# Landmarks of q and k from summed tokens: VectorE and GpSimd ahead of 16 small products, and a new order table

## The chip, the cores and the metric

The kernel runs on one core of one Trainium2 chip. The metric is the device time of one execution in microseconds, as the median of several runs. The core's engines are TensorE (PE; its weight loads are PEld), VectorE (DVE), ScalarE (ACT), GpSimd (POOL) and SyncE (SP), which work side by side, each through its own queue in order; 16 DMA engines move data.

## The reference

Eight batches of eight heads go through a Nystrom attention, and its output, 4608 rows of 512, through an MLP with squared relu. S is 576, D is 64, and m, the number of landmarks, is 32: each landmark is the mean over 18 neighbouring tokens.

```
q_lm = q.reshape(B, H, m, S // m, D).mean(axis=3)
k_lm = k.reshape(B, H, m, S // m, D).mean(axis=3)
A = sm(q, k_lm); Bm = sm(q_lm, k_lm); C = sm(q_lm, k)      # softmax of scaled scores
Z = Bm.T / (norm1(Bm) * norminf(Bm) + 1e-06)
for _ in range(6):
    Z = 2 * Z - Z @ Bm @ Z
x = (A @ Z @ C @ v)            # then heads side by side: rows of 512
out = square(maximum(x @ w_in, 0)) @ w_out                  # w_in 512x2048, w_out 2048x512
```

## The kernel before

**Layout.** A batch's q and k are loaded as bfloat16 into one buffer `kqraw`, with 96 partitions and six neighbouring tokens of each head on each partition (`c` in `[96, 2, 8, 6, 64]`); the next batch's load needs that buffer free. v has two buffers. From batch 2 on (`late`) a DMA transposition issued by SP (L420) makes `kqT` from the whole of `kqraw`; batches 0 and 1 transpose on TensorE. After the transposition a copy of one element (`seen`, L330) on GpSimd waits for it, and GpSimd then issues the load of v. All loads of q, k, v and the weights are issued by GpSimd (L331, L339, L347); stores and transpositions by SP.

**Landmarks.** Batch 0 makes them with `means` (L437) and `fold_mm`. Every later batch uses `means2` (L475): 48 products per batch with the band matrix `seg` as the weights, in groups of 32 columns; an eviction with a scale into `lmk`; `fold2_mm` (L492), four products with `ident` that bring them to the head dimension; and evictions into `kbd` (twice) and `dups["q"]`. `b_mm` (L544) makes the landmark scores in eight products that each use a quarter of the array's columns, and a softmax and six iterations follow: in each, GpSimd masks (`mask`, L579), TensorE multiplies (`step`, L640) and VectorE updates (`upd`, L651). `c_mm` (L680) and `a_mm` (L782) make the other scores. `cv_mm` (L731) takes v, `wt_mm` joins, and `g_mm` (L853) multiplies with w_in to G; with A (normalised in `a_mul`, L817, on GpSimd or VectorE), G gives the MLP's hidden layer directly.

**MLP.** `mlp_in` has 16 blocks per batch: four products (L873), a `relu` out of PSUM on ScalarE (L889) or VectorE (L891), and a `square` on ScalarE (L898) or VectorE (L900). `mlp_out` has 592 output products in all (L931), 16 to an accumulation, each then copied and stored.

**Order.** Nothing runs in the order in which it is written. `add` only records an operation with its possible engines, a cost in nanoseconds, what it reads and writes. The table `ORDER`, made ahead by a planner from these costs, is then walked by `emit`: an entry holds the operation's number (entry // 40), the engine (entry // 8 % 5: PE, ACT, DVE, POOL, SP) and the PSUM bank (entry % 8). A negative entry is a fill: products of zeros (L394), in units of 64 columns. So the costs given to `add`, the `dma=` figures among them, change nothing on the chip by themselves; what runs on which engine and in which order is in the table alone. An engine that waits for a semaphore holds up all that its queue has behind.

```
code, bank = divmod(code, 8)
idx, e = divmod(code, 5)
op, e = self.ops[idx], self.ENGINES[e]
```

Of the kernel before, what the change touches and what calls it, by code (L numbers as in the profile page):

```python
# [8 lines left out]
P = 128  # L9
# [8 lines left out]
H = 8  # L18
S = 576
# [213 lines left out]
def kernel(  # L233
# [165 lines left out]
    def constants3(e):  # L399
        nc.vector.memzero(kbd[:])  # L400
        nc.vector.memzero(cvd[:])
        for i in range(2):
            nc.vector.memzero(ECs[i][:, :, :, :, TP:P])
            nc.vector.memzero(kqTs[i][:, 2 * HT:2 * HT + M])

    add({"DVE": (1000.0,)}, constants3, writes=["kbd0", "kbd1", "cvd"])
    add({"DVE": (900.0,)}, constants2, reads=["ident", "onesf"], writes=["fold", "ones"])

    load("v", 0)

# [589 lines left out]
```

## Time and profile before

| | |
|---|---|
| time, median of 3 runs | 260.7 us (259.63 to 267.23) |
| profiled execution, its own time | 261.31 us |
| its span, first to last instruction | 259.6 us |
| granted TensorE clock | 0.999 |
| busy PE / DVE / ACT / POOL | 248.1 / 184.1 / 178.4 / 84.3 us |
| HBM read, written | 36.70 MB, 9.44 MB |

Busy time of TensorE comes from modelled ends of products that overlap, so its pace is better read from the distance between starts of products in a run. The chain of waits follows the last instruction back to what released it. A group's row gives the sum and the mean of its instructions, then the idle time of their engine just ahead of them and what ended it.

### The profile page before, as it was taken

What the parts mean: (1) busy time and instruction counts of PE and PEld (TensorE: products, weight loads), DVE (VectorE), ACT (ScalarE), POOL (GpSimd) and SP (SyncE); (2) the same over time, 40 slices, a digit from 0 to 9 for tenths busy, and PEclk for the clock granted to TensorE, in tenths of its full rate; (3) what the DMA queues carried; (4) which work ended last, traced back from release to release, by engine and by line L of the source; (5) the groups of instructions that cost most, each with busy time, mean ns of one, the idle gap of its engine ahead of it and who ended that gap; (6) DMA issues with size and microseconds to landing.
All of it is one profiled execution on the core that took longest, in us unless ns stands there. A gap on an engine that the chain in (4) does not pass through costs nothing.

```text
span 259.6 us, 7149 instructions
## 1 busy us (share of the span) xinstructions
PE 248.1 (96%) x2910; PEld 144.2 (56%) x2910; DVE 184.1 (71%) x428; ACT 178.4 (69%) x352; POOL 84.3 (32%) x127
## 2 busy tenths in 40 slices
PE   8999999999999999996999799999999999999994
PEld 2755756655555656453564376556655555645543
DVE  2289879589866997788678688887777776684300
ACT  1398988788944996786895588899857375436402
POOL 6154752604333423521474227113523530000000
PEclk9999999999999999999999999999999999999999
DMA  6999999798997999999899998989661633100405
GB/s 80 203 199 207 196 200 204 115 210 129 206 226 138 147 178 216 229 156 191 159 183 193 214 182 143 206 137 197 173 110 13 121 81 130 40 3 0 163 8 197
DMA packets 72753, 39.46 MB, mean 152 GB/s; under 512 B 45456, under 2 KB 68240, under 8 KB 72720
## 3 DMA queue, kind: packets, MB, share of 16 engines
q0 software_dynamic: 23040, 18.35, 48.0%
q1 hardware_dynamic: 49536, 20.58, 36.6%
q8 instruction: 23, 0.38, 0.6%
q14 instruction: 10, 0.08, 0.1%
q10 hardware_dynamic: 144, 0.07, 0.1%
HBM read 36.70 MB, written 9.44 MB: 178 GB/s over the span
## 4 chain that ended last, share of the span: by engine, by line
PE 66%; DMA 23%; POOL 3%; DVE 2%; issue 2%; ACT 2%; DVEq 0%; POOLq 0%; ACTq 0%
PE ps L931 37%; PE ps L873 18%; DMA kqraw<-in_q_dram 9%; DMA kqraw<-in_k_dram 7%; DMA kqT<-kqraw 4%; DMA w_out_bf<-in_moe_w_out_dram 3%; PE ps L394 3%; PE ps L853 3%; PE ps L475 1%; POOL EA L817 1%; PE ps L782 1%; PE ps L521 1%; PE ps L640 1%; POOL Pd L579 1%; PE ps L731 1%
## 5 line engine op out<-in xcount | busy, mean ns | idle before, releaser
L931 PE MATMUL ps<-w_out_bf,gs 128*128 128x512 bf16 (+2 forms) x592 | 146.8, 374 | 0.6 <-DMA w_out_bf<-in_moe_w_out_dram 0.6
L931 PEld LDWEIGHTS <-gs 128*128 128x128 bf16 x592 | 53.5, 98 | 45.2 <-issue 4.3
L873 PE MATMUL ps<-AT,G 128*128 128x288 bf16 x512 | 78.3, 286 | 0.0
L889 ACT ACTIVATE r<-ps 128x576 bf16<-128x576 f32 x88 | 54.9, 652 | 28.9 <-PE ps L873 24.5
L873 PEld LDWEIGHTS <-G 128*128 128x128 bf16 x512 | 48.3, 98 | 23.4 <-issue 0.4
L579 POOL TENSOR_TENSOR Pd<-st,ones_d 128x256 bf16<-128x256 bf16 x42 | 30.4, 725 | 70.0 <-DVE st L651 53.3
L898 ACT ACTIVATE gs<-r 128x576 bf16<-128x576 bf16 x65 | 43.9, 684 | 3.3 <-DVE r L891 2.8
L891 DVE TENSOR_SCALAR r<-ps 128x576 bf16<-128x576 f32 x40 | 30.0, 752 | 15.8 <-PE ps L873 14.2
L900 DVE TENSOR_TENSOR gs<-r 128x576 bf16<-128x576 bf16 x63 | 30.4, 494 | 4.3 <-ACT r L889 3.6
L265 ACT COPY o<-ps 128x512 f32<-128x512 f32 (+2 forms) x29 | 16.2, 571 | 14.0 <-PE ps L931 13.9
L265 ACT CAST G<-ps 128x512 bf16<-128x512 f32 x39 | 21.2, 589 | 6.2 <-PE ps L853 6.0
L817 POOL TENSOR_TENSOR EA<-EA,rA 96x384 bf16<-96x384 bf16 x20 | 16.7, 848 | 17.1 <-DVE rA L810 12.8
L651 DVE SCALAR_TENSOR_TENSOR st<-st,ps 128x128 bf16<-128x128 bf16 x40 | 11.3, 281 | 15.3 <-PE ps L640 13.7
L267 DVE CAST G<-ps 128x512 bf16<-128x512 f32 x25 | 16.8, 684 | 3.2 <-PE ps L853 3.1
L791 DVE TENSOR_REDUCE mxA<-ps 96x16 f32<-96x512 f32 x24 | 16.3, 680 | 0.9 <-PE ps L782 0.7
L800 ACT ACTIVATE EA<-SA 96x512 bf16<-96x512 f32 x24 | 14.7, 627 | 2.6 <-issue 2.1
L794 DVE TENSOR_TENSOR SA<-ps,mxA 96x512 f32<-96x512 f32 x24 | 16.1, 676 | 0.3
L394 PE MATMUL ps<-zero 128*128 128x512 bf16 (+5 forms) x48 | 14.6, 431 | 1.3 <-DVE zero L389 1.3
L806 DVE TENSOR_REDUCE sA<-EA 96x24 f32<-96x768 bf16 x16 | 14.8, 932 | 0.0
L691 ACT ACTIVATE EC<-ps,nmc 128x576 bf16<-128x576 f32 x16 | 11.8, 743 | 1.1 <-DVE nmc L686 1.0
L686 DVE TENSOR_REDUCE nmc<-ps 128x1 f32<-128x576 f32 x16 | 11.7, 748 | 1.0 <-PE ps L680 0.8
L579 POOL TENSOR_TENSOR BTd<-BTc,ones_d 128x256 bf16<-128x256 bf16 x7 | 4.7, 669 | 21.7 <-DVE BTc L267 15.7
(110 smaller groups left out, 240.6 us busy)
## 6 DMA issues: line engine op xcount, KB each, us to landing
out_dram<-o SPq DMA_DIRECT2D x35, 256.0 KB, 3.0
kqraw<-in_k_dram POOLq DMA_DIRECT2D x8, 576.0 KB, 7.2
kqraw<-in_q_dram POOLq DMA_DIRECT2D x8, 576.0 KB, 11.4
vraw<-in_v_dram POOLq DMA_DIRECT2D x8, 576.0 KB, 8.5
w_in_bf<-in_moe_w_in_dram POOLq DMA_DIRECT2D x4, 512.0 KB, 9.9
w_out_bf<-in_moe_w_out_dram POOLq DMA_DIRECT2D x4, 512.0 KB, 10.1
out_dram<-o SPq DMA_DIRECT2D x1, 192.0 KB, 2.3
kqT<-kqraw SPq DMA_TRANSPOSE x6, 8.6
```

What stands on the lines that cost most here:

```text
L265: nc.scalar.copy(dst, src)
L267: ENG[e].tensor_copy(dst, src)
L394: mm(ps[:, bank, 0:64 * w], lhsT=zero[:, 0:P], rhs=zero[:, 0:64 * w], start=True, stop=True)
L579: ENG[e].tensor_tensor(dst[:], src.unsqueeze(2).to_broadcast([P, 2, NG, M]), ones_d[:].unsqueeze(1).to_broadcast([P, 2, NG, M]), ALU.mult)
L791: add({"DVE": dve(512)}, lambda e, sa=sa, j=j: nc.vector.tensor_reduce(out=mxA[:, j, :], in_=grouped(one(sa)[0:TP, :]), axis=AX.X, op=ALU. ...
L817: ENG[e].tensor_tensor(w, w, rA[:, i, cs, :].rearrange("p c g -> p (c g)").unsqueeze(2) .to_broadcast([TP, NJ * NG, M]), ALU.mult)
L873: mm(t[:, j, 0:HALF], lhsT=G[:, i, f * P:(f + 1) * P], rhs=AT[:, i, j * HALF:(j + 1) * HALF], start=(i == 0), stop=(i == 1))
L889: nc.scalar.activation(rj, src, AF.Relu)
L891: nc.vector.tensor_scalar(out=rj, in0=src, scalar1=0.0, scalar2=None, op0=ALU.max)
L898: nc.scalar.activation(dst, r[:], AF.Square)
L900: nc.vector.tensor_tensor(dst, r[:], r[:], ALU.mult)
L931: mm(one(ok)[:, 0:hi - lo], lhsT=gs[:, f, x0:x0 + P], rhs=w_out_bf[:, f, lo:hi], start=(f == f0), stop=(f == f1 - 1))
```

## The change

For batches 2 to 7, `means2`, its eviction and `fold2_mm` are replaced. Eight `presum` operations per batch (two heads of k or of q each) add the six tokens of each partition: on VectorE one reduction and one copy, on GpSimd three additions through `half6` and `half3` in float32. `means3` then multiplies each head's sums with `seg`, eight products for k and eight for q, and three evictions write `kbd` (twice) and the q landmarks. q landmarks now lie in `qz`, a buffer that is zeroed once, at a distance at which a head's landmarks with zeros around them are a full set of weights; `b_mm` of batches 1 to 7 uses the whole array's columns and accumulates four heads. Batch 1 keeps `means2`. `square` may run on GpSimd for batches 0 and 1. DMA costs given to the planner are other figures, and `ORDER` is new throughout.

By the new table 28 of the 48 `presum` run on VectorE and 20 on GpSimd; four squares run on GpSimd, 46 on VectorE (63 before) and 78 on ScalarE (65); 32 relus on VectorE (40) and 96 on ScalarE (88); fills come to 281 units (357), the first of them 136 (160).

```
+    qz = sb.tile([P, NG * (2 * P + M)], BF16, name="qz")
+    qzd = qz.rearrange("p (g y) -> p g y", g=NG)[:, :, 0:2 * P].rearrange("p g (i x) -> p g i x", i=2)[:, :, :, 0:M]
+    kqsum = sb.tile([TP, 2, H, 2, D], BF16, name="kqsum")
...
+    add({"POOL": (1000.0,), "DVE": (380.0,)}, lambda e: ENG[e].memset(qz[:], 0.0), writes=["qz0"])
...
+        elif late:
+            mp = (A, "mp")
+            for w in range(2):
+                for x in range(H // 2):
+                    def presum(e, w=w, x=x):
+                        src = kqraw[:, w, 2 * x:2 * x + 2, :, :]
+                        dst = kqsum[:, w, 2 * x:2 * x + 2, :, :]
+                        if e == "DVE":
+                            with nc.allow_low_precision(reason="six terms, rounded once at the end"):
+                                nc.vector.reduce_sum(dst[:, :, 0, :], src.rearrange("p h c d -> p h d c"), axis=AX.X)
+                            nc.vector.tensor_copy(dst[:, :, 1, :], dst[:, :, 0, :])
+                            return
+                        nc.gpsimd.tensor_tensor(half6[:], src[:, :, 0:NJ, :], src[:, :, NJ:NC6, :], ALU.add)
+                        nc.gpsimd.tensor_tensor(half3[:], half6[:, :, 0, :], half6[:, :, 1, :], ALU.add)
+                        nc.gpsimd.tensor_tensor(dst, half3[:].unsqueeze(2).to_broadcast([TP, 2, 2, D]),
+                                                half6[:, :, 2, :].unsqueeze(2).to_broadcast([TP, 2, 2, D]), ALU.add)
+
+                    add({"DVE": (1110.0, 1190.0, 0), "POOL": (2010.0, 2010.0, 1)}, presum, reads=[("kq"[w], 0)],
+                        writes=[("sum", w, x)])
+
+                def means3(e, w=w):
+                    t = one(mp).rearrange("p (w h m) -> p w h m", w=2, m=M)
+                    for h in range(H):
+                        mm(t[:, w, h, :], lhsT=kqsum[:, w, h, :, :].rearrange("p c d -> p (c d)"),
+                           rhs=seg[:], start=True, stop=True)
...
+            for i in range(2):
+                def kbd_ev3(e, i=i):
+                    scaled(e, kbd[64 * i:64 * i + 64, :, i, :], landmarks(0, i), 1.0 / SEG)
...
+            def q_ev3(e):
+                scaled(e, qzd, landmarks(1).rearrange("p (g i) m -> p g i m", i=2), SCALE / SEG)
...
-                        mm(t[M * g:M * g + M, i, :], lhsT=dups["q"][0:D, h, :],
-                           rhs=kbd[0:D, h, 0, :], start=True, stop=True)
+                        mm(t[:, i, :], lhsT=qz[0:D, h * P:h * P + P], rhs=kbd[0:D, h, 0, :],
+                           start=(g == 0), stop=(g == NG - 1))
...
-                             dma=(8.0 * H * S * D, -4000.0, 1800.0))
+                             dma=(8.0 * H * S * D, -4000.0, 1000.0))
...
-            add({"DVE": dve(S, 2, 1), "ACT": act(S, True)}, square, reads=[("r", rn)], writes=wk)
+            sq = {"DVE": dve(S, 2, 1), "ACT": act(S, True)}
+            if b < 2:
+                sq["POOL"] = pool_tt(S)
+            add(sq, square, reads=[("r", rn)], writes=wk)
```

More of the change, by code (lines that the diff above doesn't have):

```diff
@@ L289 @@
     kbd = sb.tile([P, H, 2, M], BF16, name="kbd")
+    qz = sb.tile([P, NG * (2 * P + M)], BF16, name="qz")
+    qzd = qz.rearrange("p (g y) -> p g y", g=NG)[:, :, 0:2 * P].rearrange("p g (i x) -> p g i x", i=2)[:, :, :, 0:M]
+    kqsum = sb.tile([TP, 2, H, 2, D], BF16, name="kqsum")
+    half6 = sb.tile([TP, 2, NJ, D], F32, name="half6")
+    half3 = sb.tile([TP, 2, D], F32, name="half3")
     Eb = sb.tile([P, 2, M], F32, name="Eb")
@@ L334, in load @@
                    reads=() if behind is None else [("k", "T", behind, 0)],
-                   writes=[(nm, b % 2 if nm == "v" else 0)], dma=(4.0 * H * S * D, 1500.0, 1000.0), gate=gate)
+                   writes=[(nm, b % 2 if nm == "v" else 0)], dma=(4.1 * H * S * D, 1500.0 if b == 0 else 2300.0, 900.0), gate=gate)
     def load_w_in(j):
@@ L341, in load_wi @@
                 moe_w_in[:, j * 512:(j + 1) * 512].rearrange("(kt cp) f -> cp kt f", cp=P))
-        add({"POOL": LOAD}, load_wi, writes=[("wi", j)], dma=(4.0 * DM * 512, 1500.0, 1000.0))
+        add({"POOL": LOAD}, load_wi, writes=[("wi", j)], dma=(4.0 * DM * 512, 2000.0, 1200.0))
     def load_w_out(j, gate=()):
@@ L349, in load_wo @@
                 moe_w_out[512 * j:512 * j + 512, :].rearrange("(ft fp) c -> fp ft c", fp=P))
-        return add({"POOL": LOAD}, load_wo, writes=[("wo", j)], dma=(4.0 * DM * 512, 1500.0, 1000.0), gate=gate)
+        return add({"POOL": LOAD}, load_wo, writes=[("wo", j)], dma=(4.0 * DM * 512, 2000.0, 1200.0), gate=gate)
     nc.scalar.add_instruction(mybir.InstLoadActFuncSet(
@@ L457, in fold_ev @@
                     copy(e, dup.rearrange("p h m -> p (h m)"), one(fp)[:, 0:H * M])
-                add(either(256), fold_ev, reads=[fp], writes=[(nm, "dup")])
+                add(either(256), fold_ev, reads=[fp], writes=[(nm, "dup") if nm == "k" else (nm, "dup0")])
                 if nm == "k":
@@ L466, in attention, with landmarks @@
                             reads=[("k", "dup")], writes=["kbd%d" % i])
+        elif late:
[21 more added lines that the diff above has]
+                           rhs=seg[:], start=True, stop=True)
+                add({"PE": pe(32, 8)}, means3, reads=[("sum", w, x) for x in range(H // 2)] + ["seg"], writes=[mp],
+                    acq=None if w else ("n", mp))
+            def landmarks(w, i=None):
+                t = one(mp).rearrange("p (w h m) -> p w h m", w=2, m=M)[:, w, :, :]
+                return t if i is None else t[64 * i:64 * i + 64]
+            for i in range(2):
+                def kbd_ev3(e, i=i):
+                    scaled(e, kbd[64 * i:64 * i + 64, :, i, :], landmarks(0, i), 1.0 / SEG)
+                add(either(256), kbd_ev3, reads=[mp], writes=["kbd%d" % i])
+            def q_ev3(e):
+                scaled(e, qzd, landmarks(1).rearrange("p (g i) m -> p g i m", i=2), SCALE / SEG)
+            add(either(256), q_ev3, reads=[mp, "qz0"], writes=[("q", "dup")])
@@ L500, in q_ev @@
             def q_ev(e):
-                scaled(e, dups["q"].rearrange("p (g i) m -> p i g m", i=2), folded(1), SCALE)
+                scaled(e, qzd.rearrange("p g i m -> p i g m"), folded(1), SCALE)
             for i in range(2):
@@ L508, in attention @@
                 add(either(256), kbd_ev, reads=[fp], writes=["kbd%d" % i])
-            add(either(256), q_ev, reads=[fp], writes=[("q", "dup")])
+            add(either(256), q_ev, reads=[fp, "qz0"], writes=[("q", "dup")])
         if not late:
@@ L536, in attention @@
         bm = (A, "bm")
+        qk = ("q", "dup") if b else ("q", "dup0")
         def b_mm(e):
@@ L548, in b_mm @@
                            rhs=dups["k"][:, h, :], start=True, stop=True)
-        add({"PE": (155.0,)}, b_mm, reads=[("q", "dup"), "kbd0"] if b else [("q", "part"), ("k", "dup")], writes=[bm],
-            acq=("n", bm), mode="Q" if b else "C32")
+        add({"PE": pe(32, 8) if b else (155.0,)}, b_mm,
+            reads=[qk, "kbd0"] if b else [("q", "part"), ("k", "dup")], writes=[bm],
+            acq=("n", bm), mode="F" if b else "C32")
         sm = small
@@ L679, in c_mm @@
                     for c in range(2):
-                        mm(t[M * g:M * g + M, c, 0:HALF], lhsT=dups["q"][64 * c:64 * c + 64, 2 * g + i, :],
+                        mm(t[M * g:M * g + M, c, 0:HALF], lhsT=qz[64 * c:64 * c + 64, (2 * g + i) * P + M * g:(2 * g + i) * P + M * g + M] if b
+                           else dups["q"][64 * c:64 * c + 64, 2 * g + i, :],
                            rhs=Ts["k"][z][64 * c:64 * c + 64, 2 * g + i, :, :].rearrange("p j t -> p (j t)"),
                            start=True, stop=True)
-            add({"PE": (135.0,)}, c_mm, reads=[("q", "dup"), ("k", "T", z, 0), ("k", "T", z, 1)],
+            add({"PE": (135.0,)}, c_mm, reads=[qk, ("k", "T", z, 0), ("k", "T", z, 1)],
                 writes=[sc], acq=("h", sc), mode="Q")
@@ L718, in attention @@
                              writes=[("ECT", z, 0), ("ECT", z, 1)],
-                             dma=(800000.0, 0.0, 2600.0))
+                             dma=(800000.0, 0.0, 1100.0))
         add({"DVE": (85.0, 160.0)}, lambda e: nc.vector.reciprocal(sm["rcv"][:], sm["rsc"][:]),
@@ L829, in attention @@
                              writes=[("AT", z, 0), ("AT", z, 1)],
-                             dma=(600000.0, 0.0, 2600.0))
+                             dma=(600000.0, 0.0, 500.0))
         else:
@@ L899, in square @@
                 else:
-                    nc.vector.tensor_tensor(dst, r[:], r[:], ALU.mult)
-            add({"DVE": dve(S, 2, 1), "ACT": act(S, True)}, square, reads=[("r", rn)], writes=wk)
+                    ENG[e].tensor_tensor(dst, r[:], r[:], ALU.mult)
+            sq = {"DVE": dve(S, 2, 1), "ACT": act(S, True)}
+            if b < 2:
+                sq["POOL"] = pool_tt(S)
+            add(sq, square, reads=[("r", rn)], writes=wk)
     def store(osb, key, row, lo=0, hi=DM, ends=False):
@@ L908, in store @@
         add({"SP": (450.0,), "ACT": (450.0,)} if ends else {"SP": (450.0,)}, go, reads=[key],
-            dma=(4.0 * (hi - lo) * P, 850.0, 700.0))
+            dma=(800.0 * (hi - lo), 600.0, 400.0))
     def mlp_out(b):
```

227 rows, old and new, of the table ORDER are left out of this document.

## The prediction

> **What bounds the kernel now.** I began with the page: who is busy, and for how long.
>
> ```profile
> span 259.6 us, 7149 instructions
> PE 248.1 (96%) x2910; PEld 144.2 (56%) x2910; DVE 184.1 (71%) x428; ACT 178.4 (69%) x352; POOL 84.3 (32%) x127
> ```
>
> TensorE looks full, but ends of products are modelled here, so I priced products by the chain of waits in order of time, where a run of n products shows its true pace:
>
> ```profile
> 67.86 0.86 PE ps L931 x4
> 68.72 0.49 PE ps L873 x4
> 78.31 0.68 PE ps L475 x48
> 125.25 0.22 PE ps L492 x4
> 127.65 0.08 PE ps L544 x8
> 134.07 0.25 PE ps L782 x8
> 217.65 0.56 PE ps L853 x16
> 98.13 9.31 DMA kqT<-kqraw
> 112.66 10.93 DMA kqraw<-in_q_dram
> 123.64 0.52 PE ps L475 x24
> 136.54 11.92 DMA kqraw<-in_q_dram
> 245.93 10.41 PE ps L931 x62
> ```
>
> An output product costs 0.215 us, an input product 0.122, the 48 landmark products of a batch 0.68 together. Counted through the old order table at such prices, all products come to 238 us; the span is 259.6. About 21 us are therefore the start, the tail and waits. The chain names the waits: it leaves TensorE at 112.66 and 136.54 for a load of q, and comes back with L475, the landmark products. Their group has the sum:
>
> ```profile
> L475 PE MATMUL ps<-kqraw,seg 96*32 96x128 bf16 x336 | 6.4, 220 | 4.7 <-DMA kqraw<-in_q_dram 4.0 <-DMA kqraw<-in_k_dram 0.7
> ```
>
> TensorE takes its queue in order. At batches 5 and 6 the old table puts L475 ahead of the landing of q, so output products that need nothing from that load stand behind it: 4.7 us lost. The second thing to see is how full the two evicting engines are in the middle, from the windows:
>
> ```profile
> core 0: us, PE busy (x) PEld busy (x) DVE busy (x) ACT busy (x) POOL busy (x), PEclk, DMA share, GB/s
> 20.00:196.00 176.00, 169.41 (x2227) 100.26 (x2226) 141.31 (x334) 138.78 (x283) 67.50 (x94) 1.00 1.04 178
> 20.00:40.00 20.00, 19.01 (x337) 12.16 (x336) 17.19 (x46) 17.79 (x38) 11.38 (x15) 1.00 1.24 201
> 160.00:180.00 20.00, 20.00 (x223) 11.71 (x222) 16.67 (x37) 17.60 (x33) 3.40 (x5) 1.00 1.03 172
> ```
>
> From 20 to 196 us VectorE and ScalarE together do 280.1 us in 2 x 176: 80%. The fullest stretches have 34.98 and 34.27 of 40, 87% and 86%, with TensorE still at 19 to 20 of 20. So TensorE sets the end, with the DMA in two places, and the evicting engines are close behind.
>
> **The change, part by part.**
>
> **Products.** For each of six late batches 48 landmark products (0.68 us) and 4 folds (0.22) go: 5.4 us. They are replaced by 16 products of 32 columns. The nearest row is that of the first batch:
>
> ```profile
> 8.19 0.46 PE L437 MATMUL ps<-seg,kqraw 96*128 96x32 bf16 x12
> ```
>
> The last one's modelled end holds about 0.18, so the pace is 0.28/11 = 0.026; 16 cost 0.41, six batches 2.5. The landmark scores of seven batches go from 8 packed products (0.08) to 8 of the full array (at L782's 0.25/8, no more than 0.25): +1.1. Net -1.8.
>
> **Fills.** The table's warming products fall from 357 to 281 units of 64 columns, 0.027 us each: -2.05. All of them stand in the first 28 us, where they bridge waits of the first batch. Worth 0 if the wait stays, 2.05 if nothing else is late; I take -0.7, as about a third of an early stretch seems to be paced by TensorE rather than by the softmax and iteration chain.
>
> **The landmark wait.** In the new table the landmark products stand later, against what is left. Behind the last of them I count, for batches 5, 6 and 7: 346, 276, 212 output products and 68, 53, 35 groups of four input products, where the old table has 365, 298, 246 and 72, 64, 41. At the prices above and with the other products, 120.6, 95.0 and 68.3 us stand behind, against 128.6, 106.1 and 78.8. With q landing as before (123.6, 148.5, 172.7) and 2.5 us for the sums, the earliest chain ends would be 246.7, 246.0 and 243.5; before, 148.5 + 106.1 was already 254.6 and 256.3, the chain's end, came of it. So this wait goes: -4.7. Bounds: -4.7 and 0 (if the sums wait just as long). What is late next is not the DMA but the evicting engines.
>
> **Sums on VectorE and GpSimd.** The table gives 28 to VectorE and 20 to GpSimd; no row shows them. The rows they are built from, and those of the work that is moved to make room:
>
> ```profile
> L806 DVE TENSOR_REDUCE sA<-EA 96x24 f32<-96x768 bf16 x16 | 14.8, 932 | 0.0
> L817 POOL TENSOR_TENSOR EA<-EA,rA 96x384 bf16<-96x384 bf16 x20 | 16.7, 848 | 17.1 <-DVE rA L810 12.8 <-ACT r L889 2.8 <-ACT qdup L271 1.6
> L579 POOL TENSOR_TENSOR Pd<-st,ones_d 128x256 bf16<-128x256 bf16 x42 | 30.4, 725 | 70.0 <-DVE st L651 53.3 <-DVE st L614 16.6
> L267 DVE CAST BTc<-BTf 128x64 bf16<-128x64 f32 x7 | 1.5, 210 | 0.1
> L900 DVE TENSOR_TENSOR gs<-r 128x576 bf16<-128x576 bf16 x63 | 30.4, 494 | 4.3 <-ACT r L889 3.6
> L898 ACT ACTIVATE gs<-r 128x576 bf16<-128x576 bf16 x65 | 43.9, 684 | 3.3 <-DVE r L891 2.8
> L891 DVE TENSOR_SCALAR r<-ps 128x576 bf16<-128x576 f32 x40 | 30.0, 752 | 15.8 <-PE ps L873 14.2 <-ACT gs L898 1.0 <-ACT o L265 0.2
> L889 ACT ACTIVATE r<-ps 128x576 bf16<-128x576 f32 x88 | 54.9, 652 | 28.9 <-PE ps L873 24.5 <-issue 2.1 <-DVE cc L590 0.5
> L267 DVE CAST G<-ps 128x512 bf16<-128x512 f32 x25 | 16.8, 684 | 3.2 <-PE ps L853 3.1
> L265 ACT CAST G<-ps 128x512 bf16<-128x512 f32 x39 | 21.2, 589 | 6.2 <-PE ps L853 6.0
> L271 ACT ACTIVATE lmk<-ps 128x512 bf16<-128x512 f32 x6 | 3.6, 597 | 6.3 <-PE ps L475 6.2
> ```
>
> A VectorE sum reads 768 elements, as L806 does (0.932), and copies 128 (near 0.2): 1.13 us, 28 of them 31.6. The bound below is the copy alone plus half the reduction, 0.67, if strides came cheaper; above, twice, 2.3, if the strided read cost double. I take 1.13, since L806 reduces the same count in the same type. A GpSimd sum is three instructions of 384, 128 and 256 elements: 0.848, 0.848/2 at most, 0.725: 2.0 us, 40 in all. In return VectorE loses 17 squares (-8.4), 8 relus (-6.0), 9 evictions of G (-6.2), 2 normalisations (-1.3) and gains 5 output copies (about +3.4): with small ones +12. ScalarE gains 13 squares (+8.9), 8 relus (+5.2), 9 G (+5.3), loses 5 output copies (-2.9) and 5 lmk (-3.0): with small ones +16. GpSimd gets some 47, four squares among them (each about 576/384 x 0.848 = 1.3).
>
> Of the 28 us net on the evicting engines, 20 stand in the table where the stretch 20 to 196 lies. That stretch then holds 300.1 us. At the fullest seen, 87%, it takes 172.5 us: 3.5 less than the 176 now. TensorE alone would let it shrink by the whole 4.7. So I count **-3.5** for wait and engines together; the cover under which the sums cost nothing is used up almost exactly.
>
> **Loads.** k and q share one buffer, freed by the transposition and by the sums. One sum takes 2 us at most, a share of 8 on two engines about 4 x 1.13 or 4 x 2.0, under the 9.3 us of a transposition in the chain, so the buffer is not freed later. The last transposition, of batch 7, is issued as its q has landed:
>
> ```profile
> 172.78 5.65 SPq L420 DMA_TRANSPOSE kqT<-kqraw  x1
> ```
>
> But GpSimd also issues the loads, and a sum ahead of one holds it up 2 us. I take 0, both ways open (below, rival 4). The cost figures for DMAs in the planner's calls issue nothing.
>
> **The sum** against the profiled execution: span 259.6 - 3.5 - 1.8 - 0.7 = 253.6. Around the span lie 1.7 us (its time was 261.31), so 255.3; it stood 0.6 above the median of 260.7, so median times are spans + 1.1. Forecast: 254.7 us, 2.3% less. A difference under about 2% can't be told from none here.
>
> A rule that speaks against the change. Squares have two inputs in SBUF, and the trace shows what happens when one starts just after a GpSimd instruction:
>
> ```profile
> 57.80 0.67 POOL L579 TENSOR_TENSOR BTd<-BTc,ones_d 128x256 bf16<-128x256 bf16 x1 [7.27 <-DVE BTc L267]
> 57.82 0.96 DVE L900 TENSOR_TENSOR gs<-r 128x576 bf16<-128x576 bf16 x1
> L900 DVE TENSOR_TENSOR gs<-r x63: 390/452/959, 29.4 to 246.8; 128x576 bf16<-128x576 bf16 x63
> ```
>
> It took 0.96 where the median is 0.452; over 63 squares mean less median makes 2.6 us. With GpSimd busy 1.56 times as long and 46 squares, rows give 2.6 x 1.56 x 46/63 = 3.0, so +0.4: left in the noise. The Trainium skill (SBUF — State Buffer, Who interferes with whom) says that a VectorE instruction with two SBUF inputs and a GpSimd one that reads SBUF lock each other out for a whole instruction, while a VectorE reduction never contends. By that rule every square that meets GpSimd at work would wait half an instruction, near 0.4 us, an estimate of 46 x 0.5 x 0.4 = 9 us of VectorE's time instead of 3; shared by two engines the sum would be some 3 us higher.
>
> **The rivals.**
>
> 1. Engines don't bind: the tables pair work better and the fill goes over 87%. Then -4.7 - 1.8 - 2.05 and nothing else: span 251.1, time 252.2; with small waits gone too, 250. For it: 9.4 us of idle before the evictions of G in the groups above, which a better order could use. Against: no stretch was fuller than 87%.
>
> 2. The gain is swallowed: fill 85%, stretch 176.5. Span 259.6 + 0.5 - 1.8 - 0.7 = 257.6, time 258.7. For it: sums stand in bursts of four to six on VectorE, ahead of relus that free PSUM for input products. Against: two stretches above 85%.
>
> 3. The other side: a sum on VectorE waits for its load, in order, and relus and squares wait behind it; what was a wait of TensorE becomes one of the fuller engine. The place is the first q sum of batches 3 to 7. If the fill stays at today's 80%, the stretch takes 187.6, span 259.6 + 11.6 - 2.5 = 268.7, time 269.8. The gain is gone at a fill of 84%, and it is slower by 2% from 81.7% down. For it: a load of q takes 10.9 and 11.9 us in the chain, and at batch 6 the new table leaves 9.0 us of products between issue and first sum. Against: at the other batches it leaves 11 to 13 ahead of the first q sum on VectorE.
>
> 4. GpSimd's queue: sums ahead of the issues of k and q make each of five load cycles d later. The last q now lands at 172.7. Then the span is 172.7 + 5d + 2.5 + 68.3 + 3.3 (tail: 259.6 less the chain's 256.3) = 246.8 + 5d. It decides over the forecast from d = 1.4, is slower by 2% from d = 3.6; with two sums in front, d = 4, 266.8, time 267.9. For it: four of eight sums on GpSimd in batches 4, 5, 7. Against: most sums stand among the masks of the iteration, where GpSimd waited (70 us of idle in L579's row).
>
> That the change doesn't do what it says holds in one part: GpSimd gets 4 squares of 128, too few to matter.
>
> **How the numbers follow.** Forecast 0.40 (own range 251 to 258), rival 1 0.22, rival 2 0.20, rival 3 0.11, rival 4 0.07. Over 2% faster means under 255.5: rival 1 and about two thirds of the forecast, 0.22 + 0.27 + 0.01 = 0.50. Slower over 2% means above 265.9: 0.14, most of rivals 3 and 4. The rest, 0.36. The range goes from 248.5 (rival 1 with all small waits gone) to 264, which leaves out the upper rivals at full price.
>
> **What would show it.** Right: of the 48 old landmark products only batch 1's left, and new ones with under 1 us of idle before them at batches 5 and 6; VectorE near 196, ScalarE 194, GpSimd 131 us; fill in the middle 86 to 88%; sums at 1.1 and 2.0 us. Rival 2 or 3 shows as idle of TensorE in front of input products, released by relus, and as sums on VectorE that waited for a DMA. Rival 4 shows as the last q landing after 180 us. The forecast is wrong if the sums take 1.5 times their price, or if the idle before landmark products is still 3 us.

## The result, and the profile after

The changed kernel takes 279.49 us (277.26 to 281.34), the kernel before in the same runs 260.16: a ratio of 1.076, interval 1.063 to 1.089. The profiled span is 279.6 us. The forecast was 254.7, its range up to 264. A time is the median of all executions of a kernel; a ratio leaves out the executions in a slower state, some per cent longer at a lower granted clock, that the kernel before has too.

The page of the changed kernel, lines to be set against those of before:

```profile
span 279.6 us, 6804 instructions
PE 256.2 (92%) x2686; PEld 146.1 (52%) x2686; DVE 214.3 (77%) x446; ACT 192.4 (69%) x379; POOL 132.8 (47%) x193
PEclk9985699999999979979998999999999999999999
```

ScalarE and GpSimd came out as counted (194 and 131 were forecast). VectorE has 18 us more than the 196 forecast. The groups of the sums, of the squares that stay on VectorE, and of the new landmark products:

```profile
L485 DVE TENSOR_REDUCE kqsum<-kqraw 96x128 bf16<-96x768 bf16 x28 | 41.1, 1469 | 0.8 <-DMA kqraw<-in_q_dram 0.8
L486 DVE COPY kqsum<-kqsum 96x128 bf16<-96x128 bf16 x28 | 8.9, 319 | 1.0
L488 POOL TENSOR_TENSOR half<-kqraw 96x384 f32<-96x384 bf16 x20 | 18.7, 936 | 3.1 <-DMA kqraw<-in_k_dram 2.7
L489 POOL TENSOR_TENSOR half<-half 96x128 f32<-96x128 f32 x20 | 9.6, 479 | 1.6
L490 POOL TENSOR_TENSOR kqsum<-half,half 96x256 bf16<-96x256 f32 x20 | 15.0, 748 | 1.6
L956 DVE TENSOR_TENSOR gs<-r 128x576 bf16<-128x576 bf16 x46 | 23.0, 502 | 4.6 <-ACT r L945 4.2
L499 PE MATMUL ps<-seg,kqsum 96*128 96x32 bf16 x96 | 4.5, 178 | 8.2 <-DVE kqsum L486 4.3 <-DVE st L706 2.7 <-DVE o L1003 1.1
```

A GpSimd sum takes 0.936 + 0.479 + 0.748 = 2.16 us (2.0 forecast). A VectorE sum takes 1.469 + 0.319 = 1.79 against 1.13. TensorE now stands idle 8.2 us in front of the landmark products, and what ends it is VectorE, not a load. The shares by line of the chain of waits:

```profile
by line: PE ps L990 26.1%; PE ps L929 15.0%; DVE kqsum L485 12.6%; DMA kqraw<-in_k_dram 4.8%; DMA kqraw<-in_q_dram 3.6%; issue 3.0%; DVE r L947 2.7%; DMA AT<-EA 2.6%; DVE kqsum L486 2.3%; PE ps L909 2.1%; DVE sA L862 1.6%; PE ps L573 1.4%; 
```

The reduction alone holds 12.6% of the chain. Batch 5 shows the place. First SyncE's timeline: the transposition of q and k is issued as both have landed, here for batches 5 and 7.

```profile
137.69 5.77 SPq L429 DMA_TRANSPOSE kqT<-kqraw  x1
...
192.63 5.77 SPq L429 DMA_TRANSPOSE kqT<-kqraw  x1
```

VectorE's timeline from there on, and TensorE's at its end:

```profile
137.74 1.50 DVE L485 TENSOR_REDUCE kqsum<-kqraw 96x128 bf16<-96x768 bf16 x1
139.27 0.71 DVE L486 COPY kqsum<-kqsum 96x128 bf16<-96x128 bf16 x1
139.90 1.48 DVE L485 TENSOR_REDUCE kqsum<-kqraw 96x128 bf16<-96x768 bf16 x1
...
141.52 1.48 DVE L485 TENSOR_REDUCE kqsum<-kqraw 96x128 bf16<-96x768 bf16 x1
...
143.34 0.94 DVE L862 TENSOR_REDUCE sA<-EA 96x24 f32<-96x768 bf16 x1
144.20 1.43 DVE L485 TENSOR_REDUCE kqsum<-kqraw 96x128 bf16<-96x768 bf16 x1
145.66 0.19 DVE L486 COPY kqsum<-kqsum 96x128 bf16<-96x128 bf16 x1
```

```profile
145.91 0.34 PE L499 MATMUL ps<-seg,kqsum 96*128 96x32 bf16 x6 [1.32 <-DVE kqsum L486]
```

Four sums stand in a row on VectorE, with an update, a normalisation's sum and their copies between them. TensorE gets the last of the landmarks 8.2 us after the landing, where the forecast gave the sums 2.5. L862 (L806 before) is the instruction that the sum was priced by: 768 elements in 0.94 us, where L485 takes 1.43 to 1.50.

The windows of the changed kernel over the forecast's stretch of 20 to 196 us (busy time of PE, PEld, DVE, ACT, POOL, then the clock, the DMA's share and GB/s):

```profile
20.00:196.00 176.00, 159.21 (x1772) 91.83 (x1771) 153.12 (x312) 133.40 (x269) 102.28 (x143) 0.93 0.97 160
```

VectorE and ScalarE do 286.5 in 2 x 176, 81%, with VectorE at 87% and ScalarE at 76%. In the waits of TensorE the largest single one is new and not a sum's; it is taken up under experiments 6 to 8:

```profile
PE ps L929 <- DMA AT<-EA: 3.5, 1, 3.5
```

### The profile page after: what moved, and what is told of

It reads as the page before. It is cut to its first block, busy times and chain, and to the rows that moved or that the text cites. A ratio compares the mean times of both kernels' runs of the same rounds, so it can differ in the third digit from the quotient of the medians.

```text
span 279.6 us, 6804 instructions
## 1 busy us (share of the span) xinstructions
PE 256.2 (92%) x2686; PEld 146.1 (52%) x2686; DVE 214.3 (77%) x446; ACT 192.4 (69%) x379; POOL 132.8 (47%) x193
## 4 chain that ended last, share of the span: by engine, by line
PE 52%; DVE 31%; DMA 11%; issue 3%; POOL 1%; ACT 1%; DVEq 0%; POOLq 0%; SPq 0%
PE ps L990 26%; PE ps L929 15%; DVE kqsum L485 13%; DMA kqraw<-in_k_dram 5%; DMA kqraw<-in_q_dram 4%; DVE r L947 3%; DMA AT<-EA 3%; DVE kqsum L486 2%; PE ps L909 2%; DVE sA L862 2%; PE ps L573 1%; DVE mxA L847 1%; DVE st L706 1%; DVE nmc L742 1%; DVE gs L956 1%
## 5 line engine op out<-in xcount | busy, mean ns | idle before, releaser
L990 PE MATMUL ps<-w_out_bf,gs 128*128 128x512 bf16 (+2 forms) x592 | 151.3, 377 | 0.4 <-DVE Zd L714 0.3
L945 ACT ACTIVATE r<-ps 128x576 bf16<-128x576 f32 x96 | 61.1, 651 | 34.2 <-PE ps L929 27.7
L954 ACT ACTIVATE gs<-r 128x576 bf16<-128x576 bf16 x78 | 51.4, 681 | 5.5 <-DVE r L947 4.7
L485 DVE TENSOR_REDUCE kqsum<-kqraw 96x128 bf16<-96x768 bf16 x28 | 41.1, 1469 | 0.8 <-DMA kqraw<-in_q_dram 0.8
L947 DVE TENSOR_SCALAR r<-ps 128x576 bf16<-128x576 f32 x32 | 23.9, 754 | 10.8 <-PE ps L929 7.3
L956 DVE TENSOR_TENSOR gs<-r 128x576 bf16<-128x576 bf16 x46 | 23.0, 502 | 4.6 <-ACT r L945 4.2
L873 POOL TENSOR_TENSOR EA<-EA,rA 96x384 bf16<-96x384 bf16 x22 | 18.5, 853 | 9.6 <-DVE rA L866 7.4
L268 ACT COPY o<-ps 128x512 f32<-128x512 f32 (+1 forms) x24 | 13.5, 585 | 9.8 <-PE ps L990 9.6
L488 POOL TENSOR_TENSOR half<-kqraw 96x384 f32<-96x384 bf16 x20 | 18.7, 936 | 3.1 <-DMA kqraw<-in_k_dram 2.7
L270 DVE COPY o<-ps 128x512 f32<-128x512 f32 (+1 forms) x13 | 8.5, 653 | 11.2 <-PE ps L990 11.2
L490 POOL TENSOR_TENSOR kqsum<-half,half 96x256 bf16<-96x256 f32 x20 | 15.0, 748 | 1.6
L862 DVE TENSOR_REDUCE sA<-EA 96x24 f32<-96x768 bf16 x16 | 15.0, 941 | 0.6 <-ACT EA L856 0.6
## 6 DMA issues: line engine op xcount, KB each, us to landing
out_dram<-o SPq DMA_DIRECT2D x35, 256.0 KB, 2.6
```

Source lines behind the costliest of these rows:

```text
L268: nc.scalar.copy(dst, src)
L485: nc.vector.reduce_sum(dst[:, :, 0, :], src.rearrange("p h c d -> p h d c"), axis=AX.X)
L488: nc.gpsimd.tensor_tensor(half6[:], src[:, :, 0:NJ, :], src[:, :, NJ:NC6, :], ALU.add)
L862: add({"DVE": dve(768)}, lambda e, i=i: nc.vector.reduce_sum(sA[:, i, :, :].rearrange("p c g -> p (c g)"), EA[:, i, :, :].rearrange("p c ( ...
L945: nc.scalar.activation(rj, src, AF.Relu)
L947: nc.vector.tensor_scalar(out=rj, in0=src, scalar1=0.0, scalar2=None, op0=ALU.max)
```

## The experiments

In the expectations theory A is the time of the sums, B the clock of the start, C the new order whatever the sums cost, D the late issue of the loads, E the transpositions beside the loads, F the new order's own waits. Every ratio is to the kernel before in the same runs. "48 products" means that `means2` and its folds are back, in the new order and on its engines.

**1. No reduction on VectorE.** The sum there copies the first token and leaves out the other five.

```
-    nc.vector.reduce_sum(dst[:, :, 0, :], src.rearrange("p h c d -> p h d c"), axis=AX.X)
+    nc.vector.tensor_copy(dst[:, :, 0, :], src[:, :, 0, :])
```

> The changed kernel, but a sum on VectorE leaves out five of its six tokens: it copies the first one (and then makes the second copy as before), so the reduction of 1.47 us is a copy of about 0.2. Order, products, GpSimd's sums are the same. Theory A (VectorE's sums hold the queues: they took 1.47 + 0.32 us where 1.13 was forecast, 28 times, and 36 us of the chain are theirs): VectorE's busy time falls by about 35 us, the waits before the landmark products go, and the time falls to 257 to 264. Theory B (the granted clock alone, 0.55 from 18 to 32 us): that stretch has no sums, so the time stays at 272 or more. Theory C (the new order is bad whatever the sums cost): 270 or more.

264.78 us, ratio 1.019 (1.009 to 1.029), 0.8 us above theory A's range. Of the 19 us lost, 15 are the reductions. VectorE's busy time fell by 21.5 us (214.3 to 192.8) and not by the expected 35: the two copies take 0.38 and 0.56 us here, as most of them meet GpSimd at work (experiment 4).

**2. More fills at the start.** The page's clock row has a 5 and a 6 at 21 to 35 us, where before every slice was full.

```
 ORDER: 281 units of fills
+ORDER: 427 units, the 146 added ones between 16 and 30 us
```

> The changed kernel with some 150 units of 64 columns of fills more, all between 16 and 30 us, where TensorE waited 0.6 and 1.0 us just before the granted clock fell to one half at 19.8 us; nothing else. Theory B (clock): the clock stays at 1.00 there, the 13 us at half clock become some 7, and the time falls by 5 to 7 us, to 272 to 275. Theory A: the middle is set by VectorE's queue, which then starts earlier by the same amount, unless it waits for loads: between 0 and 5 us less. If the fills stand in the way of the first batch's chain, 0 or a loss of up to 3.

279.94 us, ratio 1.079 (1.070 to 1.088). The windows of 18 to 32 us, first of the changed kernel, then of this one:

```profile
18.00:32.00 14.00, 13.14 (x255) 8.84 (x253) 10.52 (x29) 9.64 (x20) 5.57 (x9) 0.55 1.25 206
```

```profile
18.00:32.00 14.00, 12.96 (x283) 8.44 (x282) 11.33 (x30) 10.45 (x22) 6.33 (x10) 1.00 1.25 206
```

The clock is 1.00 instead of 0.55 here and the time did not move: the half clock of this stretch decides nothing. That the added fills brought the clock back is not shown, since executions with the same 281 fills also differ there: 0.56 to 0.63 in experiments 1, 5 and 15, 0.88 in 3 and 6, 1.00 in 4, 8, 10, 11, 12, 14 and 16. Two stretches in the middle of the changed kernel, 98 to 105 us (0.76) and 119 to 126 us (0.79), were not tried.

**3. The 48 products in the new order,** without any sum.

```
-    presum(...)                     # the eight sums of a batch
-    means3(...)                     # 16 products of 32 columns
+    means2(bank); fold2()           # at the place of the last sum and of means3
```

> The changed kernel's order and engines, q landmarks in the zeroed buffer and scores in the full array, but no sums: the 48 landmark products, the eviction on ScalarE and the 4 folds of the kernel before stand where the last sum of each batch stood. Theory A: without 48 us of VectorE and 40 of GpSimd, against 1.8 us of TensorE more, the time falls to 255 to 265. Theory C: it stays at 270 or more. Theory B: at least 268, since the early stretch is the same.

266.72 us, ratio 1.025 (1.014 to 1.037). Without one sum the new order is slower than the old, and 2 us above theory A's range, where theory C had 270 or more. The waits for q of before are gone, but in this kernel's chain of waits stands

```profile
79.35 9.57 DMA kqT<-kqraw
```

and TensorE waits 3.3 us for it ahead of A's scores.

**4. Three additions in place of the reduction.**

```
-    nc.vector.reduce_sum(...); nc.vector.tensor_copy(...)
+    nc.vector.tensor_tensor(hv6[:], src[:, :, 0:NJ, :], src[:, :, NJ:NC6, :], ALU.add)
+    nc.vector.tensor_tensor(hv3[:], hv6[:, :, 0, :], hv6[:, :, 1, :], ALU.add)
+    nc.vector.tensor_tensor(dst, <hv3 twice>, <hv6's third pair twice>, ALU.add)
```

> The changed kernel, but a sum on VectorE is made as GpSimd makes it, in three additions (384, 128 and 256 elements) with bfloat16 between them, which read along the row and not with a step of 64 elements. By the squares (576 elements in 0.45) they should take 0.35 + 0.2 + 0.3, so 0.85 to 1.0 us instead of 1.79, more where GpSimd is at work at the same time. Theory A: VectorE loses some 22 us and the time falls to 262 to 270. Theories B and C: 276 or more.

274.14 us, ratio 1.054 (1.042 to 1.066): only 5 us better. The group of the last addition in the tile's view (minimum, median, maximum in ns):

```profile
L489 DVE TENSOR_TENSOR kqsum<-hv,hv x28: 286/738/1235, 47.7 to 196.5; 96x256 bf16<-96x256 bf16 x28
```

Of the 28, 13 run beside no GpSimd instruction and take 0.286 to 0.289 us each; the 15 that overlap one take 0.66 to 1.24. One of these, with the GpSimd instruction that starts just ahead of it:

```profile
74.67 0.91 POOL L492 TENSOR_TENSOR half<-kqraw 96x384 f32<-96x384 bf16 x1
74.70 1.02 DVE L489 TENSOR_TENSOR kqsum<-hv,hv 96x256 bf16<-96x256 bf16 x1
```

So the one locks the other out, which is the rule that the prediction weighed (the Trainium skill, SBUF — State Buffer, Who interferes with whom).

**5. The sum along the row.** The same reduction with its six terms next to each other; it adds neighbouring values instead of the six tokens.

```
-    src.rearrange("p h c d -> p h d c")                       # terms 64 elements apart
+    src.rearrange("p h c d -> p h (c d)").rearrange("p h (d c) -> p h d c", c=NC6)
```

> The changed kernel, but VectorE's reduction adds six neighbours along the row (of the same 768 elements, to the same 128 results) instead of six that lie 64 elements apart, so it leaves out the right grouping and nothing else. Theory A1 (the step was the mis-sized term): the reduction takes 0.93 us as the forecast had it, not 1.47; VectorE does 15 us less and the time falls to 266 to 272, and what is left above 255 is not the price of the sum. Theory A2 (the count of elements sets the price, and the shorter L806 was of another kind): 1.4 us still, and no change.

263.98 us, ratio 1.015 (0.995 to 1.035), 2 us below theory A1's range. Its group:

```profile
L485 DVE TENSOR_REDUCE kqsum<-kqraw 96x128 bf16<-96x768 bf16 x28 | 26.2, 936 | 5.1 <-DMA kqraw<-in_q_dram 4.3 <-DMA kqraw<-in_k_dram 0.8
```

0.936, the forecast's price to the hundredth. So the step between the terms costs 0.53 us a sum, 15 us of VectorE in 28, and 15.5 us of time. With the forecast's own price the kernel takes 264, not 254.7: that is not the whole of the error. Experiment 1, with no reduction at all, is no faster (264.8).

**6. The 48 products with earlier loads:** loads of v, k and q of a cycle issued together, at the place of the first of them on GpSimd.

```
 ORDER:  ... v q mask mask k ...     (batch 3, issues at 65 to 71 us)
+ORDER:  ... k v q mask mask ...
```

> The new order with the 48 old products and no sums (266.7 us), and now GpSimd's loads of k, v and q stand together, each three at the first of their three places, ahead of the masks, normalisations and squares that stood between them. In the run without this the last of k and q landed at 79.3, 105.4, 129.0, 155.3 and 177.4 us, in the kernel before at 72.1, 98.0, 123.6, 148.5 and 172.6. Theory D (GpSimd's queue of the new table holds the loads up, and that is what the order loses): landings 3 to 6 us earlier, time 260 to 263. Theory E (the new table leaves too little time behind the transpositions, whatever the loads do): waits of products for transpositions stay, and 265 to 268.

269.4 us, ratio 1.033 (1.016 to 1.050), not better than experiment 3. The q and k of batches 3 to 6 landed 2 to 7 us earlier than there, those of batch 7 2.8 us later. Two transpositions of A now stand in the chain of waits:

```profile
83.47 7.65 DMA AT<-EA
111.84 12.38 DMA AT<-EA
```

**7. The kernel before, landmarks of batches 5 and 6 later** by some 3 us of output and input products: the forecast's "landmark wait" taken away alone.

```
 ORDER of before: output products and input groups behind the landmark products
-  batch 5: 381 and 72;  batch 6: 314 and 64
+  batch 5: 373 and 70;  batch 6: 313 and 59
```

(counted from the first entry of the operation, not from its last product).

> The kernel before with one thing moved in its table: the landmark products of batches 5 and 6, their evictions, folds and scores stand 3 to 4 us and 2 to 3 us of products later, so that the loads of q have landed when TensorE comes to them (it waited 2.3 and 1.7 us there, and 0.4 for k). If such a wait is worth its full length, as the forecast had it, the time is 256 to 258, 3 to 5 us under the kernel before. If the softmax behind them is then late, or the next load, no change.

262.82 us, ratio 1.012 (1.001 to 1.024): no gain. TensorE no longer waits for q. Its largest wait in the profiled execution is now

```profile
PE ps L872 <- DMA AT<-EA: 3.0, 1, 3.0
```

and the chain has

```profile
106.02 10.94 DMA AT<-EA
```

The edit did not bring this wait. It ends ahead of the first entry in which the two tables differ, and the moved landmark products come only after it, as TensorE's timeline shows:

```profile
117.00 3.37 PE L872 MATMUL ps<-AT,G 128*128 128x288 bf16 x16 [2.98 <-DMA AT<-EA]
127.80 0.41 PE L474 MATMUL ps<-kqraw,seg 96*32 96x128 bf16 x16
```

The same instructions fell out otherwise in the kernel before: there A's transposition was issued at 107.0, ahead of the loads of v (107.7) and k (109.8), and took 5.4 us; here it is issued at 106.0, behind v (105.5) and ahead of k (107.5), and takes 10.9. Even without these 3.0 us the profiled execution (264.4) would stand at 261, not at 256 to 258. Why the wait that was taken away shows in no time stays open.

**8. The changed kernel with the earlier loads of experiment 6.**

```
 ORDER:  ... v q mask mask k ...
+ORDER:  ... k v q mask mask ...
```

> The changed kernel, sums and all, with GpSimd's loads of k, v and q together at the first of their three places. Theory D: landings up to 10 us earlier by batch 7 and 268 to 274. Theory A: the landmarks lag the landing by 8 to 14 us because of VectorE's sums, which then come no faster: 275 to 280.

283.69 us, ratio 1.092 (1.082 to 1.103), slower still. The landings of batches 3, 4 and 6 come 5 us earlier, but those of batches 5 and 7 some 2.5 us later, so that the early last landing of theory D did not come about. TensorE waits 6.4 us for one transposition of A, which is again in the chain:

```profile
89.84 11.58 DMA AT<-EA
```

**9 to 12. Less traffic: v.** Seven eighths of the v loads of batches 2 to 7 are left out, in the kernel before, in the 48 products, in the changed kernel and in the sum along the row.

```
+    if nm == "v" and b >= 2:
+        nc.gpsimd.dma_start(dst[:, 0:1, :, :], src[b][0:1].rearrange("h (p c) d -> p h c d", c=NC6))
+        return
```

> The kernel before with seven eighths of the v loads of batches 2 to 7 left out (one head is loaded, the other seven stay those of batches 0 and 1). Theory E: what the new order costs without the sums (5 to 6 us) are the transpositions that run beside the loads; the v load is the one that lies beside them. Then the kernel before, whose order leaves the transpositions 7 to 12 us, gains little from less traffic: 257 to 260. Rival F: the new order pairs the evicting engines worse, and the DMA has nothing to do with it: the same 257 to 260 here. This run is the base for the two others.

256.0 us, ratio 0.981 (0.972 to 0.990). The old order gains some 5 us where 1 to 4 were expected: the waits for q go, as the forecast priced them (4.7).

> The 48 products in the new order (266.7 before) with the same seven eighths of v left out. Theory E: A, C and k-q transpositions fall from up to 12 us to 3 to 6, the waits of input and landmark-score products behind them go, and the time falls by 4 to 6 us to 260 to 263, within 3 us of the kernel before with the same cut. Rival F: transpositions get faster and the time stays 5 us above the kernel before with the same cut: 263 to 266.

268.5 us, ratio 1.026 (1.015 to 1.037): no gain. A's transposition still runs beside the load of k (7.5 of its 7.9 us) and what is left of v, and TensorE waits 3.9 us for it:

```profile
82.37 7.86 DMA AT<-EA
```

> The changed kernel (279.5) with the same cut of v. Theory E: it gains the 4 to 6 us that the 48 products in this order gain, and the sums' 13 us stay: 273 to 276. Rival F: 277 to 280. If it falls to under 270, the sums cost only by what they delay on the DMA, against the run without the reduction.

271.92 us, ratio 1.043 (1.033 to 1.053): 7.6 us less than with full loads, more than expected.

> The sums along the row (264.0; they add neighbouring values instead of the six tokens) with the same cut of v. This is the forecast's own price of a sum and little traffic beside the transpositions. Theory E: 258 to 261, level with the kernel before with the same cut. Rival F: 262 to 265. Under 257 the change would pay once both costs are gone.

265.91 us, but from 259.96 (in theory E's range) to 267.85 (above rival F's), without a ratio: inconclusive.

**13 to 16. Less traffic: all.** The same four with q, k and v of batches 2 to 7 cut to one head of eight, `if b >= 2` in place of the condition above. These are compared with each other, since the kernel before scattered from 257.7 to 264.6 beside them.

> The kernel before with seven eighths of the loads of q, k and v of batches 2 to 7 left out (one head is loaded, the others keep the values of earlier batches). With the v loads alone so cut it came to 256.0. All remaining waits of TensorE for q are gone and the transpositions run alone: 254 to 256. Base for the three others.

255.66 us (255.25 to 255.77): 5 us under the 260.7 of the kernel before, 2 to 4 under the two best executions beside it (257.7 and 259.3). So much the loads cost it, save the eighth that is still loaded.

> The 48 products in the new order with the loads of q, k and v so cut. Theory E2: what was left with small v (268.5, 12 us above the same order of before) is A's transposition beside the loads of k and q, 7.9 us long there: it falls to 3 us, and the time to 258 to 262. Rival F, the new order waits on its own engines: 265 to 268.

260.89 us (260.8 to 261.1). A's transposition at 82 us takes 3.5 us, as E2 has it, and the time is 7.6 us less than in experiment 10. What is left, 5.2 us above the old order with the same cut, is the new order's own.

> The changed kernel with the loads of q, k and v so cut. If the sums cost by the landings that they delay and wait for, the time falls to within 2 us of the 48 products in the new order with the same cut. If they cost by VectorE's time and place, it stays 4 us or more above it, with TensorE still idle before the landmark products.

272.09 us (269.34 to 274.19): 11 us above the 48 products so cut, and no less than with v alone cut (271.92). The windows of 100 to 140 us and of 20 to 196 us, and the group of the products:

```profile
100.00:140.00 40.00, 35.84 (x406) 21.50 (x410) 38.70 (x72) 32.87 (x66) 27.88 (x41) 1.00 0.66 139
20.00:196.00 176.00, 161.20 (x1796) 94.74 (x1818) 160.50 (x323) 139.03 (x280) 100.54 (x148) 0.95 0.61 117
```

```profile
L502 PE MATMUL ps<-seg,kqsum 96*128 96x32 bf16 x96 | 4.5, 177 | 7.7 <-DVE kqsum L489 4.3 <-DVE st L709 2.1 <-DVE o L1006 1.1
```

VectorE is busy 38.7 of 40 us, and the idle time ahead of the landmark products is 7.7, as with full loads (8.2).

> The sums along the row, which add neighbouring values instead of the six tokens, with the loads so cut: the forecast's price of a sum, and no load in the way. Theory E2: 254 to 258, level with the kernel before so cut. Rival F: 260 to 264.

258.37 us (257.67 to 259.09), 0.4 us above E2's range and 2.7 above the kernel before so cut. The same windows and the same group here:

```profile
100.00:140.00 40.00, 38.16 (x453) 22.39 (x458) 37.78 (x87) 32.19 (x68) 27.73 (x43) 1.00 0.53 111
20.00:196.00 176.00, 169.72 (x1983) 99.14 (x2012) 161.02 (x356) 148.65 (x303) 108.15 (x159) 1.00 0.63 124
```

```profile
L502 PE MATMUL ps<-seg,kqsum 96*128 96x32 bf16 x96 | 3.8, 177 | 0.8 <-DVE kqsum L489 0.7
```

In the program only the step between the terms differs from experiment 15, and 6.9 of the 7.7 us of idle and 13.7 us of the time are gone (11 to 16 by the single executions of experiment 15; its profiled one also has a clock of 0.56 from 18 to 32 us, this one 1.00). VectorE is almost as full in both, 160.5 and 161.0 of 176 us, but in the same stretch TensorE gets through 1983 products here and 1796 there.

## Why the prediction was wrong, step by step

From the kernel before to the changed one by the last four runs. Each row between the first and the last is a difference of two medians, so the rows add up by construction; those with experiment 15 or with full loads are sure to some 3 us.

| | us |
|---|---|
| kernel before, loads cut (13) | 255.7 |
| new order and engines, full-array scores, still 48 products (14 less 13) | +5.2 |
| sums at the forecast's price in place of the 48 products (16 less 14) | -2.5 |
| the step between the sums' terms (15 less 16) | +13.7 |
| full loads (279.5 less 15; the kernel before pays 2 to 5) | +7.4 |
| changed kernel | 279.5 |

**The price of a VectorE sum failed, and it is most of the error.** "I take 1.13, since L806 reduces the same count in the same type": count and type are the same, the distance between terms is not. 1.79 was inside the bounds (0.67 to 2.3), but the range of the time was not carried to that end of them. 28 x 0.66 = 18 us is just what VectorE has over its forecast. Of the 0.66, 0.53 is the step between the terms; taken away, it gave 15.5 us of time (13.7 with loads cut). The rest is the copy, 0.32 for 0.2. A rule that spoke against the change was passed over here: the Trainium skill (SBUF — State Buffer, Door 1: The DMA port swizzle) says in a note that SBUF has lines of 16 bytes, and that each access which goes to a new line pays. The terms lie 64 elements of two bytes apart, so every access does. The runs agree with its direction: 1.469 against 0.936 us for the same 768 elements. That the lines are the cause of the step's price, no run here shows.

**One pool for both evicting engines hid where the excess would lie.** The forecast put 28 us into the two and asked how full they can be together, 87%. At its own price of a sum, with loads cut, that came out: in experiment 16 the two do 309.7 of 352 us from 20 to 196 us, 88%, and TensorE is busy 169.7 of 176. With full loads (experiment 5) it is 300.5 of 352, 85%. With the true price the excess lies on one engine. The forecast's own working then gives 300.1 + 18.5 = 318.6 us in the stretch; at 87% that is 183 us, 7 more than before, at the 81% seen in the window it is 197. VectorE is at 91% in experiments 15 and 16 alike, and the 13 us more that it has to do in 15 (214.1 against 201.1) come out as time nearly whole. At the forecast's price the sums cost nothing that shows: experiment 1 is no faster than 5, and 14, without any sum, is slower than 16.

**"2.5 us for the sums" behind a landing failed.** It is 8.2 us at batch 5 and 13.7 at batch 7 (192.6 to 206.4). But the delay alone is not what costs: at batch 5 of experiment 16 it is 12.2 us (114.8 to 127.1), and TensorE is idle for 0.8 us in all ahead of the landmark products, having other products to do. The number of products behind was right: from the end of the last landmark products at 206.9 to the end at 279.6 are 72.7 us, where the forecast had 68.3 and a tail of 3.3.

**"I take 0" for the loads failed, mostly as a consequence.** The last q and k are transposed at 192.6 instead of 172.8, past the 180 that rival 4 named. With nothing but the step between the terms taken away it is 176.2 (5), and with loads cut the same step moves it from 176.2 (15) to 160.6 (16): some 16 of the 20 us come from the price of the sums. Moving the issues (6, 8) did not bring the last landing forward, so what late loads cost by themselves was not measured.

**The landmark wait of -4.7 had the right size and is not shown as a gain.** With less traffic the waits for q go and the old order gets some 5 us by experiment 9 (2 to 5 by 13). With the products placed later the wait goes too, and no time is gained (7); the cause is open, since the wait for A's transposition in that profile lies ahead of the change. In the new order the waits for q are gone as forecast (3), and DMA transpositions of 7 to 12 us stand in the chain instead (of q and k in 3, of A in 6, 8 and 10). The forecast took their durations as fixed and named the evicting engines as late next, "not the DMA".

**Products: right as far as seen.** Sixteen new products take 0.39 us in the chain (0.41 forecast), eight of the new scores 0.29 (at most 0.25). -5.4 + 2.5 = -2.9 were counted for sums in place of the 48 products, and experiments 14 and 16 differ by 2.5; that difference also holds whatever the sums cost at the forecast's price. **Fills:** the -0.7 shows nowhere; 146 units more change nothing either (2). **Squares:** 502 ns, as by the row (494 before). By the prediction's estimate from the skill's rule of the lock they would have taken 0.2 us more each. Of the 46, 29 overlap no GpSimd instruction and take 0.41 to 0.46; of the other 17 only five take over 0.5, up to 1.13. The 2.4 us that the mean makes over the median is near the 3.0 that the prediction took from rows. In the copies and in experiment 4 the lock shows more.

**The rivals.** Rivals 3 (269.8) and 4 (267.9) came nearest, both too low. Rival 4 has its landing after 180 us, but as a consequence of the sums' price. Rival 3 has the fill (80%) and the sign, but its mechanism, sums that wait for their load, is not what happened: L485 waited 0.8 us for loads in all.

**Open** is also what the 5.2 us of the new order consist of. With loads cut no wait of TensorE in experiment 14 is longer than 1.3 us; there are many small ones, and some belong to how the 48 products were put into this order. It wasn't tried further.

## What to carry to other kernels

Price an instruction by a row with the same access pattern, not only the same count and type; where only a contiguous row exists and the new one strides, carry both bounds through to the range of the time. Ask of each added piece of work which single engine gets it and whether it stands between a landing and TensorE: an average over two engines hides that. A wait that is gone is not yet time gained (7): try it in an experiment of its own, and before the next wait in the profile is taken as the effect of an edit, look whether it lies behind the first entry that the edit changed.

## What the runs showed of the hardware

- A VectorE reduction of 768 bfloat16 values on 96 partitions takes 0.936 us with neighbouring terms and 1.469 with terms 128 bytes apart.
- The copy behind it is stretched and the reduction is not (the tile's view of the changed kernel, minimum, median, maximum in ns):

```profile
L485 DVE TENSOR_REDUCE kqsum<-kqraw x28: 1349/1478/1504, 50.5 to 203.1; 96x128 bf16<-96x768 bf16 x28
L486 DVE COPY kqsum<-kqsum x28: 191/192/881, 52.1 to 204.6; 96x128 bf16<-96x128 bf16 x28
```

  Of the 28 copies, 13 overlap no GpSimd instruction and take 0.19 us each; of the 15 that do, eight take 0.47 to 0.88. With experiment 4's additions (0.29 us alone, 0.66 to 1.24 beside GpSimd) this agrees with the Trainium skill (SBUF — State Buffer, Who interferes with whom), by which copies and two-input instructions can be locked out by GpSimd and reductions are not.
- The transposition of A by DMA takes 3.0 to 5.1 us with no load of GpSimd's beside it, and up to 12.4 us beside such loads (7.9, 10.9, 11.6 and 12.4 in experiments 10, 7, 8 and 6). The same entries of the table can fall either way: 5.4 us in the kernel before, 10.9 in experiment 7.
- The granted clock from 18 to 32 us was between 0.55 and 1.00 in executions with the same fills and the same order up to there; 0.55 against 1.00 (the changed kernel, and experiment 2 with more fills) made no time that could be measured.
